# A decode block with its backward pass: the value contraction is issued ahead of the score-gradient chain, the exponential is placed first on ScalarE, and VectorE shares PSUM evacuation from the last step on

## Chip, cores and metric

The kernel runs on one core of a Trainium2 chip. The metric is the device time of one launch in microseconds (us), taken as the median of several runs; lower is better.

## What is computed

The reference is a residual block for one token of each of two sequences, `x + A(xn) + B(xn)`, and the gradients of it with respect to every input. A is attention over a cache with grouped heads, B is a gated bilinear layer.

```python
B, Sq, D = 2, 1, 576;  Hq, Hkv, Sk, Dh = 32, 16, 4096, 128;  F = 4608      # bfloat16
xn = layernorm(x)
q  = xn @ wq                                   # 32 heads; two query heads share one K/V head
p  = softmax((q . k_cache) * Dh**-0.5);  o = p @ v_cache
A  = o @ wo
B  = ((xn @ w_gate) * (xn @ w_up)) @ w_down
out = x + A + B
# returned: out, and by jax.vjp with grad_out the gradients of
# x, k_cache, v_cache, wq, wo, w_gate, w_up, w_down
```

The gradients of the caches are as large as the caches: k_cache and v_cache are 2 x 16 x 4096 x 128 values each, 32 heads of 1 MB for each of the two. Each head has to be read once and a gradient of the same size written once. Reads and writes are 92.5 MB each in all, with the weights.

## The kernel before

**Steps.** The main loop has 16 steps, n = 0 to 15. A step handles one batch row and two K/V heads with their four query rows. Four steps make a group, which shares one slice of `wq` and `wo`. A step does this:

- *Scores of K.* `slot` loads a K head (1 MB, `head_load`, L541, on SP's queue), transposes it in two halves on VectorE (`head_scores`, tile X, L141; 1.2 us a half) and multiplies it on TensorE into a PSUM tile `ps_sc`.
- *Softmax.* `by_rows` copies the scores out (VectorE, L565) and transposes them (TensorE, L569); then come the row maximum (L626), the maximum over the row group (L630, L632), the negated bias `negb` (VectorE, L635), the exponential `ex` with its row sum `z` (ScalarE, L641), the sum over the group (TensorE, L643), its reciprocal `rz` (VectorE, L645), the probabilities `pr` (L648) and their transpose `pT` (a tile rowT).
- *Scores of V.* The same with the V heads, for the gradient of the probabilities: four more half-head transposes and matmul blocks into `dp_ps`.
- *`dscores`.* `by_rows` again, the row sums `cs` (L661), the correction `cr` (L668), the score gradient `ds` (L669) and its transpose `dsT`.
- *Contractions.* `end_of_V` (L802) sums the V rows with the probabilities: 64 matmuls that read both V heads as they were loaded, a copy `o_sb` (L588), one small matmul (L591), a copy into `oT`. It needs `pT` and not `ds`. `end_of_K` (L797) does the same with `dsT` and the K heads; it is traced in the next step.
- *Outer products.* The gradients of K and V: `masked` (GpSimd, L597) spreads `pr` and `ds` into `prm` and `dsm`, `build_bd` (GpSimd, L532) spreads a query row into `bd`, and `outer_units` multiplies them in pairs of matmuls into a PSUM tile `ps_o`, evacuates each pair (1024 columns, 256 KB) into a quarter of a tile `so` and stores each full `so` (1 MB) from GpSimd's queue (L618). 16 pairs in a step are for the outer products of K and V.

Units of the gated layer (`mlp_units`, in nine of the steps) and of the gradients of `wq` and `wo` (`back_units`, after each group) wait in a list `side` and are interleaved. Their outputs pass through `ps_o` and tiles `stw`, `std`, `stt`, `sto`, `stq`, `stqt`.

**Evacuation.** `evac` (L116) sends a PSUM copy either to VectorE (L121) or to ScalarE (L124). It keeps an estimate of the load of each engine in `load`, to which `dve()` and `act()` add other work. VectorE is allowed only once `ending` is filled, which is after the last step; before that all these copies go to ScalarE.

**Order.** Instructions are put in order at build time by a list scheduler: each engine then runs its queue strictly in that order. `tc.high_priority()` lets an instruction go ahead of others that are ready at that point of the schedule. The matmuls of a `Block` are kept together (all carry the line L105).

**Buffers.** Loaded heads and weights share 12 slots (tag `nat`), output tiles share 5 (tag `st`), so a load on SP's queue waits until a contraction has freed a slot, and a copy into a new output tile waits until an earlier store has landed. PSUM has two `ps_o`, two score tiles (tag `sc`) and two small tiles (tag `m`). Once `ending` is filled, every third pair uses the two score tiles (`ps_x`) instead of a `ps_o`.

**End.** After step 15, `end_of_K`, the outer products left over, `back_units` of the last group and `final_units` (the output `out`, and the gradient of x: a chain of some ten small VectorE instructions, L835 to L873) are interleaved in the order of `side`.

Of the kernel before, what the change touches and what calls it, by code (L numbers as in the profile page):

```python
# [8 lines left out]
AF = mybir.ActivationFunctionType  # L9
# [7 lines left out]
def view(t, p0, np_, off, dims):  # L17

    (pstep, _), *_ = t.ap
    return bass.AP(t.tensor, t.offset + p0 * pstep + off, [[pstep, np_], *[list(d) for d in dims]])  # L20
# [3 lines left out]
def kernel(  # L24
# [22 lines left out]
    nc = tc.nc  # L47
# [10 lines left out]
    NIT = NGRP * Bq * 2  # L58
    NCH = Sk // P
    WW = 48 + P  # L60
    SCALE = float(Dh) ** -0.5
# [12 lines left out]
    def ps_m(shape, dtype=FP32):  # L74
        return ps.tile(list(shape), dtype, tag="m", bufs=2, name="ps_m")

    def ps_sc():
        return ps.tile([P, P], FP32, tag="sc", bufs=2, name="ps_sc")
# [3 lines left out]

    pairs_made = [0]
    ending = []

    def ps_pair():

        pairs_made[0] += 1
        if ending and pairs_made[0] % 3 == 0:
            o = [ps.tile([P, 512], FP32, tag="sc", bufs=2, name="ps_x") for _ in range(2)]  # L90
            return [t[:] for t in o], None
        o = ps_o()
        return [o[:, 0, :], o[:, 1, :]], o
# [20 lines left out]
    load = {"v": 0.0, "s": 0.0}  # L114

    def evac(out, in_, cols):  # L116
        cv = 0.16 + cols * 0.00104
        cs = 0.19 + cols * 0.00083
        if ending and load["v"] + cv < load["s"] + cs:
            load["v"] += cv  # L120
            nc.vector.tensor_copy(out=out, in_=in_)  # L121
        else:
            load["s"] += cs
            nc.scalar.copy(out, in_)  # L124
# [7 lines left out]
                evac(out(a), view_in(o[a]), cols // 2)  # L132

    def dve(us):
        load["v"] += us

    def act(us):
        load["s"] += us

    def t32(out, in_):  # L140
        nc.vector.transpose(out, in_)  # L141
# [370 lines left out]
    def build_W(st, b, s, t):  # L512
        for a in range(4):
            nc.gpsimd.tensor_copy(  # L514
                view(W[t][:], 32 * a, 32, 48 + 4 * a, [[2 * WW, 4], [WW + 2, 2], [1, 2]]),
                view(st["rep"][:], 32 * a, 32, t * 4 * GH * 2 + 8 * s + b, [[GH * 2, 4], [4, 2], [2, 2]]),
            )
# [18 lines left out]
    def small(name, shape=(P, 1), dtype=FP32, bufs=2):  # L536
        return sb.tile(list(shape), dtype, tag=name, bufs=bufs, name=name)
# [24 lines left out]
    def by_rows(t_ps):  # L562

        s_sb = small("s_sb", (P, P), FP32, 1)
        nc.vector.tensor_copy(s_sb[:].rearrange("p (a c m) -> p a c m", a=4, c=8),  # L565
                              view(t_ps[:], 0, P, 0, [[4, 4], [16, 8], [1, 4]]))
        act(0.35)
        s_ps = ps_sc()
        nc.tensor.transpose(s_ps[:], s_sb[:], identf[:])  # L569
        return s_ps  # L570
# [52 lines left out]
    def softmax(s_ps):  # L623
        s_ps = by_rows(s_ps)
        mx = small("mx")
        nc.vector.reduce_max(mx[:], s_ps[:], axis=AX.X)  # L626
        mT = ps_m([1, P])
        nc.tensor.transpose(mT[:], mx[:], identf[:])
        m4 = small("m4", (1, 4))
        nc.vector.reduce_max(m4[:], mT[0:1, :].rearrange("o (a m) -> o m a", m=4), axis=AX.X)  # L630
        nb_ps = ps_m([P, 4])
        nc.tensor.matmul(nb_ps[:], lhsT=ones[:], rhs=m4[:], start=True, stop=True)  # L632
        negb = small("negb")
        nb4 = small("nb4", (P, 4), FP32, 1)
        nc.vector.tensor_tensor_reduce(  # L635
            out=nb4[:], in0=nb_ps[:], in1=R4[:], scale=-SCALE, scalar=0.0,
            op0=ALU.mult, op1=ALU.add, accum_out=negb[:],
        )
        ex = small("ex", (P, P), FP32, 1)
        z = small("z")  # L640
        nc.scalar.activation(ex[:], s_ps[:], AF.Exp, bias=negb[:], scale=SCALE, accum_out=z[:])  # L641
        z_ps = ps_m([P, 1])
        nc.tensor.matmul(z_ps[:], lhsT=G4[:].rearrange("p a m -> p (a m)"), rhs=z[:], start=True, stop=True)  # L643
        rz = small("rz")
        nc.vector.reciprocal(rz[:], z_ps[:])  # L645

        pr = small("pr", (P, P), BF16)
        nc.vector.tensor_scalar(pr[:].rearrange("p (j c) -> p j c", c=4), view(ex[:], 0, P, 0, [[1, 32], [32, 4]]),  # L648
                                rz[:], None, op0=ALU.mult)
        pT = rowT[0][n_rows[0] % 2]  # L650
        n_rows[0] += 1
        t32(pT[:, 0:P], view(pr[:], 0, P, 0, [[1, 4], [4, 32]]))
        dve(0.3 + 0.3 + 0.3 + 0.2 + 0.2 + 0.25 + 0.25)
        act(0.5)
        return pr, pT, ex, rz

    def dscores(pr, ex, rz, dp_ps):
        dp_ps = by_rows(dp_ps)
        ds = small("ds", (P, P), BF16)
        cs = small("cs")  # L660
        nc.vector.tensor_tensor_reduce(  # L661
            out=ds[:], in0=ex[:], in1=dp_ps[:], scale=1.0, scalar=0.0,
            op0=ALU.mult, op1=ALU.add, accum_out=cs[:],
        )
        c_ps = ps_m([P, 1])
        nc.tensor.matmul(c_ps[:], lhsT=G4[:].rearrange("p a m -> p (a m)"), rhs=cs[:], start=True, stop=True)
        cr = small("cr")
        nc.vector.tensor_tensor(cr[:], c_ps[:], rz[:], ALU.mult)  # L668
        nc.vector.scalar_tensor_tensor(  # L669
            out=ds[:].rearrange("p (j c) -> p j c", c=4), in0=view(dp_ps[:], 0, P, 0, [[1, 32], [32, 4]]),  # L670
            scalar=cr[:], in1=pr[:].rearrange("p (j c) -> p j c", c=4), op0=ALU.subtract, op1=ALU.mult)
        dsT = rowT[1][n_rows[1] % 2]
        n_rows[1] += 1
        t32(dsT[:, 0:P], view(ds[:], 0, P, 0, [[1, 4], [4, 32]]))
        dve(0.3 * 2 + 0.2 + 0.25)
        return ds, dsT
# [95 lines left out]
    side = []  # L772
# [11 lines left out]
    def slot(src, t, b, l, s_ps, per, mid=None):  # L784
        n = head_load(src, b, l)
        head_scores(n, t, l % 2, s_ps, 0)
        more(2)
        if mid:
            mid()
        head_scores(n, t, l % 2, s_ps, 1)  # L790
        more(2)
        other(per)
        return n
# [6 lines left out]
    def end_of_V(st, b, s, V, pT):  # L800
        t_ps = contract(pT, V)
        nc.vector.tensor_copy(st["oT"][:, 0, 4 * s:4 * s + 4, b], t_ps[:])  # L802
        dve(0.2)

    def step(n):
        g, k = divmod(n, 4)
        return g, k // 2, k % 2
# [70 lines left out]
    final = final_units()  # L878
# [4 lines left out]
    st = group_front(0, *loaded)  # L883
# [3 lines left out]
    for n in range(NIT):  # L887
        g, b, s = step(n)
        l0 = G * g + 2 * s
        side += plan.get(n, [])[1:]  # L890
        per = max(1, -(-len(side) // 4))
        new = n + 1 < NIT and step(n + 1)[0] != g
        K, V = [], []
        if new:
            loaded = group_loads(g + 1)
        s_ps = ps_sc()
        for x in range(2):
            K.append(slot(kview, 0, b, l0 + x, s_ps, per, (lambda: end_of_K(*last[:5])) if x == 0 and last else None))
            if x == 0:
                if last:  # L900
                    outs += outer_units(last[5], last[6], last[1], G * last[0]["g"] + 2 * last[2], okview)
                    if last[0]["g"] != g:
                        side[0:0] = back_units(last[0])
                        per = -(-len(side) // 4)
                bd1 = build_bd(st, b, s, 1)
        pr, pT, ex, rz = softmax(s_ps)
        prm = masked(pr, "prm")
        if n + 1 < NIT and not new:
            build_W(st, *step(n + 1)[1:], 0)
        dp_ps = ps_sc()  # L910
        for x in range(2):
            if x == 1 and n + 1 in plan:
                plan[n + 1][0][0]()
            V.append(slot(vview, 1, b, l0 + x, dp_ps, per))
            if x == 0:
                outs += outer_units(prm, bd1, b, l0, ovview)
                bd0 = build_bd(st, b, s, 0)
                if new:
                    nxt = group_front(g + 1, *loaded)
                    build_W(nxt, 0, 0, 0)  # L920
        if n + 1 < NIT:
            build_W(nxt if new else st, *step(n + 1)[1:], 1)
        ds, dsT = dscores(pr, ex, rz, dp_ps)
        dsm = masked(ds, "dsm")
        end_of_V(st, b, s, V, pT)
        last = (st, b, s, K, dsT, dsm, bd0)
        if new:
            st = nxt
# [3 lines left out]
    end_of_K(*last[:5])  # L932
    outs += outer_units(last[5], last[6], last[1], G * last[0]["g"] + 2 * last[2], okview)
    units = back_units(last[0])
    side += final[:1] + units[:2] + final[1:] + units[2:]
    while outs or side:
        more(2)
        other(1)
# [30 lines left out]
```

## Time and profile before

| | |
|---|---|
| median of 5 runs | 499.01 us (495.48 to 500.01) |
| profiled execution: its time, its span | 502.08 us, 500.3 us |
| busy: TensorE, ScalarE, VectorE, GpSimd | 77%, 70%, 65%, 53% of the span |
| DMA: reads queue, writes queue | 48.4%, 46.7% of 16 engines' span |
| moved | 186.06 MB, mean 372 GB/s |
| one 1024-column evacuation | ScalarE 1.02 us (mean of 249); VectorE 1.22 to 1.23 us |
| load of one head, issue to landing (median) | 12.9 us (K), 16.7 us (V) |
| last 1 MB store issued, last GpSimd store issued, end | 483.0 us, 493.7 us, 500.3 us |

The profile lists for each engine what it did and, for the idle time ahead of an instruction, which other engine's work ended it. Times are counted from the start of the span. A GB/s figure for a stretch of time says what all 16 DMA engines moved in it. No compute engine is busy throughout, and the DMA rate changes from stretch to stretch, so the stages have to be read one by one.

### The profile page before, as it was taken

To read this page: it belongs to the slowest core of one execution; us is meant where nothing else is said; L and a number is where in the kernel's file an instruction comes from. 1 tells how busy PE (TensorE), PEld (TensorE's weight loads), DVE (VectorE), ACT (ScalarE), POOL (GpSimd) and SP (SyncE) were. 2 spreads that over 40 slices of the span, in tenths; PEclk is the share of its full clock that TensorE was granted. 3 is DMA by queue.
4 is the path that set the end of the run, shared out by engine and by line. 5 is a ranking of instruction groups with operands and counts; after the bars stand their busy time and mean duration, and the time that the engine had idled before them with its cause. 6 is when DMAs were issued, how large, how long until landed. Compare 5 with 4: busy or idle time off the path is not lost.

```text
span 500.3 us, 16989 instructions
## 1 busy us (share of the span) xinstructions
PE 383.1 (77%) x7344; PEld 260.1 (52%) x7417; DVE 327.1 (65%) x680; ACT 348.4 (70%) x439; POOL 264.6 (53%) x404
## 2 busy tenths in 40 slices
PE   2777879867878888488998868668888678888843
PEld 1665656544655565366665446445656446564510
DVE  6786784942858686465787565566678474884383
ACT  4143867848757877477986768757787678899843
POOL 3245356743646474456547346547557246587613
PEclk9865988979989898878999879978999878999995
DMA  7998999999799999989999999999999999996765
GB/s 252 384 399 311 355 416 397 420 420 404 273 389 391 421 415 402 422 330 392 383 418 405 419 419 352 418 395 395 366 384 408 414 422 332 420 390 236 261 257 189
DMA packets 52900, 186.06 MB, mean 372 GB/s; under 512 B 4141, under 2 KB 19129, under 8 KB 44633
## 3 DMA queue, kind: packets, MB, share of 16 engines
q1 hardware_dynamic: 28392, 92.49, 48.4%
q0 software_dynamic: 24432, 92.48, 46.7%
q8 instruction: 58, 0.95, 0.7%
q14 instruction: 18, 0.14, 0.1%
HBM read 92.48 MB, written 92.48 MB: 370 GB/s over the span
## 4 chain that ended last, share of the span: by engine, by line
PE 32%; DMA 26%; DVE 12%; ACT 11%; issue 8%; POOL 4%; another core or an unknown queue 0%; POOLq 0%; ACTq 0%; SPq 0%; DVEq 0%
DMA out_dram<-so 14%; PE ps_o L105 13%; DMA kv<-in_A_k_cache_dram 9%; PE ps_m L105 9%; ACT so L124 9%; PE ps_sc L105 5%; DVE X L141 5%; DMA wgu<-in_B_w_gate_dram 3%; DVE Xw L141 2%; POOL prm L597 1%; PE ps_m L591 1%; ACT std L124 1%; POOL bd L532 1%; POOL out_dram L764 1%; ACT stw L124 1%
## 5 line engine op out<-in xcount | busy, mean ns | idle before, releaser
L124 ACT CAST so<-ps_o 128x1024 bf16<-128x1024 f32 x249 | 238.8, 1023 | 67.3 <-PE ps_o L105 26.0
L141 DVE STREAM_TRANSPOSE X<-kv 128x1024 f32<-128x1024 f32 x128 | 157.4, 1233 | 38.8 <-DMA kv<-in_A_k_cache_dram 16.0
L105 PEld LDWEIGHTS <-X 128*128 128x128 bf16 x2048 | 81.7, 103 | 33.0 <-DVE X L141 14.6
L105 PE MATMUL ps_sc<-W,X 128*128 128x64 bf16 (+1 forms) x2048 | 89.8, 200 | 7.7 <-DVE X L141 4.6
L105 PE MATMUL ps_o<-bd,prm 128*128 128x512 bf16 x212 | 74.5, 428 | 16.6 <-ACT so L124 5.6
L618 POOL DMA_DIRECT2D out_dram<-so x64 | 50.2, 784 | 69.7 <-ACT so L124 49.5
L105 PE MATMUL ps_o<-bd,dsm 128*128 128x512 bf16 x219 | 71.9, 399 | 10.1 <-ACT so L124 7.2
L532 POOL TENSOR_TENSOR bd<-dense,maskq 128x1024 bf16<-128x1024 bf16 x32 | 60.6, 1894 | 15.1 <-DVE dense L529 10.9
L124 ACT CAST stw<-ps_o 128x1024 bf16<-128x1024 f32 x36 | 34.7, 1016 | 16.2 <-PE ps_o L105 6.7
L124 ACT CAST std<-ps_o 128x576 bf16<-128x576 f32 x36 | 21.4, 644 | 32.9 <-PE ps_o L105 27.1
L105 PEld LDWEIGHTS <-prm 128*128 128x128 bf16 x256 | 22.5, 105 | 32.4 <-issue 20.1
L514 POOL COPY W<-rep 32x16 bf16<-32x16 bf16 x128 | 25.2, 197 | 26.6 <-PE ps_sc L105 18.8
L105 PE MATMUL ps_m<-kv,rowT 128*32 128x128 bf16 x2048 | 36.8, 226 | 1.5 <-issue 1.3
L597 POOL TENSOR_TENSOR prm<-pr,maskc 128x1024 bf16<-128x1024 bf16 x16 | 30.3, 1892 | 14.2 <-DVE pr L648 13.5
L105 PEld LDWEIGHTS <-dsm 128*128 128x128 bf16 x256 | 21.6, 103 | 27.5 <-issue 20.5
L105 PEld LDWEIGHTS <-rowT 128*32 128x32 bf16 x2048 | 30.6, 100 | 5.9 <-issue 4.4
L597 POOL TENSOR_TENSOR dsm<-ds,maskc 128x1024 bf16<-128x1024 bf16 x16 | 30.4, 1901 | 5.7 <-DVE ds L669 5.4
L105 PEld LDWEIGHTS <-Wdy 128*128 128x128 bf16 x306 | 22.8, 110 | 7.9 <-DVE Xo L141 2.9
L124 ACT CAST sto<-ps_o 128x576 bf16<-128x576 f32 x27 | 16.5, 650 | 13.7 <-PE ps_o L105 12.4
L141 DVE STREAM_TRANSPOSE Xw<-wgu 128x1152 f32<-128x1152 f32 x18 | 24.2, 1354 | 2.0 <-PE ps_sc L105 2.0
L105 PEld LDWEIGHTS <-xnr 32*128 32x128 bf16 (+1 forms) x440 | 12.8, 97 | 20.3 <-issue 15.6
L414 POOL DMA_DIRECT2D out_dram<-stw x18 | 13.9, 772 | 16.2 <-ACT stw L124 16.2
(186 smaller groups left out, 553.6 us busy)
## 6 DMA issues: line engine op xcount, KB each, us to landing
out_dram<-so POOLq DMA_DIRECT2D x64, 1024.0 KB, 12.4
kv<-in_A_k_cache_dram SPq DMA_DIRECT2D x32, 1024.0 KB, 12.9
kv<-in_A_v_cache_dram SPq DMA_DIRECT2D x32, 1024.0 KB, 16.7
out_dram<-stw POOLq DMA_DIRECT2D x18, 512.0 KB, 10.7
wd<-in_B_w_down_dram SPq DMA_DIRECT2D x9, 576.0 KB, 5.3
out_dram<-std POOLq DMA_DIRECT2D x9, 576.0 KB, 9.0
wo<-in_A_wo_dram SPq DMA_DIRECT2D x4, 1152.0 KB, 12.8
wgu<-in_B_w_gate_dram SPq DMA_DIRECT2D x9, 512.0 KB, 14.4
```

Of the source, the lines that this page charges most:

```text
L105: ins = nc.tensor.matmul(*args, **kwargs)
L124: nc.scalar.copy(out, in_)
L141: nc.vector.transpose(out, in_)
L414: nc.gpsimd.dma_start(out[0:512, f0:f0 + FS].rearrange("(c p) n -> p c n", p=P), st[:])
L514: nc.gpsimd.tensor_copy(view(W[t][:], 32 * a, 32, 48 + 4 * a, [[2 * WW, 4], [WW + 2, 2], [1, 2]]), view(st["rep"][:], 32 * a, 32, t * 4 * ...
L532: nc.gpsimd.tensor_tensor(bd[:], view(dense[:], 0, P, 0, [[Dh, 2], [0, 4], [1, Dh]]), view(maskq[:], 0, P, 0, [[0, 2], [1, 4], [0, Dh]]), ...
L591: nc.tensor.matmul(t_ps[:], lhsT=o_sb[:], rhs=RV[:].rearrange("p x r -> p (x r)"), start=True, stop=True)
L597: nc.gpsimd.tensor_tensor(m[:], view(rows[:], 0, P, 0, [[0, 8], [1, P]]), view(maskc[:], 0, P, 0, [[1, 8], [0, P]]), ALU.mult)
L618: nc.gpsimd.dma_start(oview[b, :, :, l0 + x].rearrange("a m n -> m a n"), st[:].rearrange("p a c d -> p a (c d)"))
L764: nc.gpsimd.dma_start(out_5[r0:r0 + 4 * P, :].rearrange("(h p) n -> p h n", p=P), m["so"][:])
```

## The change

Four edits. First, in `softmax` the exponential is issued with high priority. Second, `end_of_V` is traced ahead of `dscores` and `masked`. Third, a second flag `both` is set at the start of step 15, with the load estimates set to zero; from there on `evac` may choose VectorE, and `dve()` no longer adds to VectorE's estimate once `ending` is filled. Fourth, at the end the last unit of `final_units` (the gradient of x) is placed behind the four pairs of units that make the gradient of `wo` (`outer_o`), instead of ahead of them.

```diff
-        if ending and load["v"] + cv < load["s"] + cs:
+        if both and load["v"] + cv < load["s"] + cs:
             load["v"] += cv
             nc.vector.tensor_copy(out=out, in_=in_)
...
     def dve(us):
-        load["v"] += us
+        if not ending:
+            load["v"] += us
...
-        nc.scalar.activation(ex[:], s_ps[:], AF.Exp, bias=negb[:], scale=SCALE, accum_out=z[:])
+        with tc.high_priority():
+            nc.scalar.activation(ex[:], s_ps[:], AF.Exp, bias=negb[:], scale=SCALE, accum_out=z[:])
...
         side += plan.get(n, [])[1:]
+        if n == NIT - 1:
+            both.append(1)
+            load["v"] = load["s"] = 0.0
...
+        end_of_V(st, b, s, V, pT)
         ds, dsT = dscores(pr, ex, rz, dp_ps)
         dsm = masked(ds, "dsm")
-        end_of_V(st, b, s, V, pT)
...
-    side += final[:1] + units[:2] + final[1:] + units[2:]
+    side += final[:1] + units[:2] + final[1:3] + units[2:6] + final[3:] + units[6:]
```

More of the change, by code (lines that the diff above doesn't have):

```diff
@@ L84 @@
     ending = []
+    both = []
     def ps_pair():
```

## The prediction

> **What bounds the kernel now.** I read the page first: shares of the engines, then the DMA rate in 40 slices.
>
> ```profile
> PE 383.1 (77%) x7344; PEld 260.1 (52%) x7417; DVE 327.1 (65%) x680; ACT 348.4 (70%) x439; POOL 264.6 (53%) x404
> ...
> DMA  7998999999799999989999999999999999996765
> GB/s 252 384 399 311 355 416 397 420 420 404 273 389 391 421 415 402 422 330 392 383 418 405 419 419 352 418 395 395 366 384 408 414 422 332 420 390 236 261 257 189
> ```
>
> No compute engine is full, while DMA is near its best rate (415 to 422 GB/s) in many slices. 186 MB at 415 GB/s are 448 us of a 500.3 us span. What can be won lies where the rate is below that: in dips about once or twice a group, and in the last 50 us. The windows view of those stretches:
>
> ```profile
> 48.00:60.00 12.00, 11.11 (x278) 7.99 (x284) 8.30 (x16) 10.39 (x13) 4.00 (x8) 0.98 0.88 333
> 128.00:142.00 14.00, 10.86 (x279) 8.28 (x280) 12.96 (x24) 9.45 (x10) 8.23 (x20) 1.00 0.80 278
> 220.00:228.00 8.00, 7.37 (x223) 5.38 (x224) 5.57 (x13) 7.03 (x9) 6.48 (x5) 1.00 0.79 264
> 304.00:312.00 8.00, 6.74 (x173) 4.88 (x174) 3.20 (x6) 7.37 (x10) 3.87 (x6) 1.00 1.01 330
> 360.00:372.00 12.00, 11.31 (x279) 7.73 (x272) 8.33 (x17) 9.97 (x11) 6.69 (x8) 1.00 0.96 351
> 420.00:428.00 8.00, 6.57 (x169) 4.87 (x171) 2.83 (x8) 7.38 (x9) 4.56 (x6) 1.00 0.94 318
> 448.00:500.30 52.30, 32.90 (x446) 16.26 (x450) 28.15 (x58) 33.96 (x46) 25.11 (x28) 0.86 0.67 242
> ```
>
> The last column is GB/s. Against 415, a stretch of length w loses w x (1 - rate/415): 2.4, 4.6, 2.9, 1.6, 1.9, 1.9, and 21.8 us in the last. Why the dips are there is told by the waits of SP's queue, which issues the loads (waited for: total, times, longest):
>
> ```profile
> SPq L337 <- PE ps_m L105: 56.4, 5, 20.1
> ...
> SPq L541 <- PE ps_m L105: 32.4, 13, 7.0
> ```
>
> The load of `wd` and the heads behind it wait for a contraction (tile ps_m) to free a slot: in step 3 `wd` is issued at 134.75, just after the V contraction began (133.63). So I asked what holds that contraction, in the timeline of PE in step 3:
>
> ```profile
> 115.25 0.38 PE L632 MATMUL ps_m<-m,ones 1*128 1x4 f32 x2
> 116.02 0.59 PE L105 MATMUL ps_o<-bd,prm 128*128 128x512 bf16 x2 [0.40 <-ACT so L124]
> ...
> 122.44 0.59 PE L105 MATMUL ps_o<-bd,dsm 128*128 128x512 bf16 x2 [0.32 <-ACT so L124]
> 122.87 0.30 PE L643 MATMUL ps_m<-z,G 128*128 128x1 f32 x2
> ```
>
> Pairs for the outer products stand between the two small matmuls of the softmax, 0.92 us each because ScalarE evacuates them, and the exponential (122.20) stands behind the same copies on ScalarE, although its bias was ready at 115.75. Step 15 has the same picture; the timelines of ACT and DVE:
>
> ```profile
> 453.39 7.43 ACT L124 CAST so<-ps_o 128x1024 bf16<-128x1024 f32 x8 [0.24 <-PE ps_o L105]
> 460.67 0.41 ACT L641 ACTIVATE ex<-ps_sc,negb 128x128 f32<-128x128 f32 x1
> ...
> 453.74 0.08 DVE L635 DVE_READ_ACCUMULATOR2_ANT negb<- 128x1 f32 x1
> ...
> 461.21 0.29 DVE L661 CUSTOM_DVE_ANT_0 ds<-ex,ps_sc 128x128 bf16<-128x128 f32 x1 [5.92 <-ACT ex L641]
> ```
>
> The exponential could start at 453.8 and starts at 460.67; VectorE idles 5.92 us for it. From about 450 no head is left to load, and the rate falls: the end is set by chains.
>
> **Part 1, the exponential.** By the timelines it is late behind its bias by 6.45 us in step 3, 1.8 in 6, 4.8 in 9, 1.75 in 10, 4.2 in 13, 1.8 in 14, 6.9 in 15, and at most 1.2 elsewhere. In the order of instructions of the changed kernel it stands 4 copies earlier in step 3, 2 in steps 6, 9 and 13, 3 in 7, 10, 11 and 14, 8 in 15, and 2 or 3 later in steps 2 and 4. Step 3: 4 x 0.92 = 3.7 us. Steps 9 and 13: the first of four 0.55 us copies waits for a store until 294.52 and 411.45, and stays ahead; 2 x 0.55 = 1.1 us each. Steps 6, 10, 14: 1.1 to 1.8. Step 15: the whole 6.8. The copies it overtakes come 0.6 us later (0.41 and the read of the sum, 0.24); the queue behind them has that slack, since ScalarE idles 30% of the span. Steps 2 and 4 lose at most 2 and 3 copies of 0.6 to 1 us; in 4 the copies precede a bias that comes late anyway (153.71, behind a load), so I take nothing.
>
> **Part 2, the V contraction.** In the changed order the pairs between the bias matmul and the V contraction fall from 17 to 6 in step 3, from 12 to 3 in steps 7 and 11, from 7 to 3, 5, 5 in 6, 9, 13. At 0.92 us a pair, less what the exponential still holds, the V slots come free 7 to 8 us sooner in 3, 7, 11 and, by the rows of step 9 (the sum's matmul behind 3 pairs instead of 5, so `rz` 2.1 us sooner, and `pT` made ahead of a 1.4 us transpose instead of behind it), about 3.4 us sooner in 9 and 13: loads issued at 302.94 and 419.45 move to 299.5 and 416. But something is moved back. On VectorE `cr`, `ds` and `dsT` now stand behind three to six transposes of the next heads (step 6: 1 to 5 before `dsT`; step 10: 2 to 5; 1.2 us each), so the K contraction and the two slots that it frees come later: 1 to 2 us in steps 0, 2, 3, 5, 6, 8, 10, 12, about 12 us summed, and 1 to 3 us sooner in 4, 7, 9, 11, 13. GpSimd's `dsm` and the K outer products follow it; SP's order of issue is unchanged.
>
> What this is worth before 411 us: the dips there lose 13.4 us. A load takes 12.9 us from issue to landing, though 1 MB at 415 GB/s is 2.5, so some 10 us of queued transfers cover a slot that comes 1 or 2 us late; outside the dips an earlier slot wins nothing for the same reason. Best case: the dips fed by V slots close (2.9 + 1.6 + 1.9) and a third of that of step 3 (1.6): -8. Worst: the late K slots meet an empty queue in most of their steps: +10. I take -2, near nothing, since V sooner and K later alternate.
>
> From 411.45 ScalarE no longer waits for stores of a backlog, and steps 13 and 14 are a chain: -1.1 for the exponential, -3.4 for V, -1 for K, later ordering against it in 14: I take -2 (between -3.4 and +1).
>
> [...]
>
> **Part 3, VectorE evacuates from step 15 on.** The changed order has six more copies on VectorE: four `so` of 1.22 us and one `ps_x` of 0.65, a `sto` of 0.74 instead of one of 0.44, one `stqt` of 0.68, in all 6 us with the overlap of neighbours taken off. `exp` to `Wm` (the step that starts the last group's gradients) took 460.67 to 471.43. It now starts 6.8 us sooner, and two `so` copies stand inside the chain, between the V and K copies into `oT`, in place of two `ps_x` behind it: +1.0. So `Wm` at 465.6. From there VectorE had 16.9 us of work and 4.0 of gaps to its last copy (492.37). It gets 5.1 more, and fills most gaps: 22.0 + 1.3 = 23.3, last copy at 488.9, that is -3.5 us. With no gap left -5; with all of them -1. The rest (7.9 us from the last copy to the end of the span: two stores, their landing, the close) stays. ScalarE's list ends sooner than VectorE's, so VectorE sets the end. On GpSimd `prm`, `bd` and the preparation of the last units (0.66 + 0.66 + 2.30 us) now stand ahead of three stores around 445 to 451; the slots of these are wanted only near 457, so I take nothing; without that cover it is 3.6 us.
>
> **Part 4, the order of the last units.** The gradient of x goes behind the `sto` copies, so the two `sto` stores leave before the small chain, not at 488.54. They are not the last transfer: inside part 3.
>
> **Sum.** -2 - 2 - 3.5 = -7.5: 502.08 becomes 494.6 for the profiled execution, which lies 3.1 above the median. On the median: 499.0 - 7.5 = 491.5; for this case alone 486 to 494.
>
> **Rivals.**
> - *The dips close.* For: every dip lies behind a late contraction. Against: K slots come later in eight steps. -8 - 3.4 - 4.5: 483.
> - *VectorE eats the gain.* For: its estimate no longer counts its own work at the end, and it gets 5 us more behind `Wm`; two copies of 1.2 us sit inside the chain. Against: 15 us of gaps after 455. Parts 1 to 3 give -2: 497.
> - *K slots late: slower.* VectorE runs in order, so `cr` waits behind transposes that themselves wait for a load that waits for a slot. For: VectorE waits 16 us in all for K loads now. Against: these heads were issued 20 us or more before use outside the dips. It decides once six of the eight late steps lose 2 us each: +12, less 5.5 kept at the end: 505.5.
> - *The exponential blocks ScalarE*, standing at its head with the bias not ready. It did so in steps 0, 2, 4, 7 and 11 already (late by at most 0.2): a few us, inside the range.
>
> **How the numbers follow.** Forecast 0.45, dips close 0.17, VectorE eats it 0.25, slower 0.13. Range 482 to 501: both nearest rivals are in, and 2 in 10 outside, most of it above. A measurement of this kernel tells about 1% from no change (494.0 to 504.0). Faster by over 1%: 0.6; within 1%: 0.28; slower: 0.12.
>
> **What would show it.** The exponential of step 15 within 1 us of its bias, and VectorE's idle time for `ex` gone; `wd` issued 7 us sooner after the bias of step 3, and K contractions 1 to 2 us later behind `rz` in steps 6 and 10; rates above 300 in the six windows; VectorE's last copy about 8 us before the end of the span, with ScalarE done before it. Wrong if VectorE shows new waits for K loads ahead of `cr`, if the six windows stay below 300, or if the last VectorE copy is no sooner, counted from the last bias.

## The result, and the profile after

The changed kernel took 497.58 us (median of 36 runs, 491.60 to 504.01), the kernel before in the same comparisons 499.38 (71 runs). The ratio is 0.9952, with a 95% interval of 0.9933 to 0.9970: 2.4 us faster, where 7.5 were forecast. The ratio takes only the runs within 1.5% of the fastest of their kernel, so it is not the quotient of the two medians. The profiled execution took 497.36 us (span 495.5), which is its median; that of before lay 2.7 above its own, so the two spans differ by more than the kernels do, and the ratios are what counts below. Sums over a profile, here and below, are those of one execution each.

The page of the changed kernel, with the shares of the engines and the transfer rows in 40 slices:

```profile
PE 386.0 (78%) x7338; PEld 264.1 (53%) x7417; DVE 332.2 (67%) x686; ACT 343.9 (69%) x433; POOL 265.3 (54%) x404
...
DMA  8999999999999999997999999999899999977695
GB/s 248 380 390 379 415 408 401 418 420 406 412 412 410 420 410 413 418 415 267 367 413 384 419 414 306 419 413 405 295 410 400 393 417 392 401 276 266 257 341 191
```

The dips of before have gone from where they were and stand elsewhere: 267, 306 and 295 GB/s. The windows view shows both, first the stretches of the prediction (the last one up to the new end), then three new ones:

```profile
48.00:60.00 12.00, 10.48 (x268) 7.34 (x269) 7.84 (x17) 9.46 (x12) 6.36 (x13) 1.00 1.01 414
128.00:142.00 14.00, 11.76 (x276) 7.80 (x277) 11.03 (x22) 12.17 (x15) 8.08 (x16) 1.00 1.02 417
220.00:228.00 8.00, 6.30 (x71) 4.46 (x71) 1.73 (x9) 4.57 (x7) 0.80 (x1) 0.50 0.95 362
304.00:312.00 8.00, 5.75 (x71) 3.62 (x73) 4.14 (x9) 5.70 (x9) 2.57 (x4) 1.00 1.02 391
360.00:372.00 12.00, 11.69 (x224) 6.97 (x224) 9.28 (x14) 11.68 (x14) 5.92 (x11) 1.00 1.02 408
420.00:428.00 8.00, 6.93 (x102) 4.60 (x103) 5.50 (x11) 7.40 (x11) 2.80 (x5) 1.00 1.01 387
448.00:495.50 47.50, 30.78 (x416) 15.60 (x419) 30.57 (x61) 28.74 (x39) 22.59 (x25) 0.86 0.76 275
...
230.00:240.00 10.00, 8.64 (x201) 6.05 (x203) 8.78 (x17) 8.95 (x10) 8.50 (x17) 1.00 0.72 227
296.00:304.00 8.00, 6.64 (x211) 5.26 (x210) 3.44 (x9) 5.98 (x7) 6.18 (x10) 0.90 0.84 266
350.00:360.00 10.00, 8.88 (x219) 6.31 (x220) 8.57 (x18) 8.97 (x10) 7.55 (x15) 1.00 0.79 280
```

Adding up the slices of the GB/s row (each rate by a 40th of the span), before had moved 55.2 MB by 150 us and after 58.6; by 425 us it was 164.1 and 166.2; by 450 us 174.2 and 174.1. The lead of 8 us of transfer that stands at 150 us, after step 3, is all given back before the end.

Where a part of it goes is seen in step 7. Its row maximum `mx` is done at 212.5 instead of 227.6, but the bias only at 223.8 instead of 231.1: 11.3 us for what took 3.5. The timelines of ScalarE, TensorE and VectorE there:

```profile
220.05 1.93 ACT L125 CAST so<-ps_o 128x1024 bf16<-128x1024 f32 x2 [5.25 <-DMA out_dram<-so]
...
221.11 1.01 PE L106 MATMUL ps_o<-bd,prm 128*128 128x512 bf16 x2 [4.95 <-ACT so L125]
221.92 0.42 PE L630 MATMUL ps_m<-identf,mx 128*1 128x128 f32 x1
...
222.37 0.28 DVE L632 TENSOR_REDUCE m<-ps_m 1x4 f32<-1x128 f32 x1 [6.16 <-PE ps_m L630]
```

Read from the top: ScalarE has no output tile free until a store lands, the pair on TensorE has no PSUM tile `ps_o` free until ScalarE copies, the transpose of the row maximum stands behind that pair in TensorE's queue, and VectorE waits 6.16 us for it. In the waits view this kind of wait grew from 7.4 us (3 times) to

```profile
ACT so L125 <- DMA out_dram<-so: 28.6, 9, 5.3
```

(total, times, longest), while VectorE's waits for K loads, 16.0 us before, fell to 1.3. Waits for loads were traded for waits for stores.

### The profile page after: what moved, and what is told of

It reads as the page before. It is cut to its first block, busy times and chain, and to the rows that moved or that the text cites. A ratio compares the mean times of both kernels' runs of the same rounds, so it can differ in the third digit from the quotient of the medians.

```text
span 495.5 us, 16979 instructions
## 1 busy us (share of the span) xinstructions
PE 386.0 (78%) x7338; PEld 264.1 (53%) x7417; DVE 332.2 (67%) x686; ACT 343.9 (69%) x433; POOL 265.3 (54%) x404
## 4 chain that ended last, share of the span: by engine, by line
DMA 32%; PE 25%; DVE 12%; ACT 11%; issue 9%; POOL 6%; DVEq 0%; POOLq 0%; ACTq 0%
DMA out_dram<-so 29%; PE ps_o L106 9%; PE ps_m L106 9%; ACT so L125 9%; DVE X L143 5%; PE ps_sc L106 3%; DMA out_dram<-stw 3%; POOL bd L534 2%; POOL dsm L599 2%; DVE Xw L143 1%; ACT sto L125 1%; POOL prm L599 1%; ACT std L125 1%; DVE so L122 1%; PE ps_m L646 1%
## 5 line engine op out<-in xcount | busy, mean ns | idle before, releaser
L125 ACT CAST so<-ps_o 128x1024 bf16<-128x1024 f32 x245 | 235.0, 1019 | 88.1 <-DMA out_dram<-so 28.6
L143 DVE STREAM_TRANSPOSE X<-kv 128x1024 f32<-128x1024 f32 x128 | 156.1, 1227 | 25.4 <-PE ps_sc L106 16.2
L106 PEld LDWEIGHTS <-X 128*128 128x128 bf16 x2048 | 80.7, 102 | 25.7 <-DVE X L143 9.9
L106 PE MATMUL ps_sc<-W,X 128*128 128x64 bf16 (+1 forms) x2048 | 88.6, 199 | 4.9 <-DVE X L143 3.5
L106 PE MATMUL ps_o<-bd,dsm 128*128 128x512 bf16 x210 | 67.3, 391 | 12.9 <-ACT so L125 9.5
L106 PE MATMUL ps_m<-kv,rowT 128*32 128x128 bf16 x2048 | 42.0, 246 | 3.0 <-DVE rowT L143 2.7
L106 PEld LDWEIGHTS <-rowT 128*32 128x32 bf16 x2048 | 35.7, 111 | 12.7 <-DVE rowT L143 7.6
L125 ACT CAST std<-ps_o 128x576 bf16<-128x576 f32 x36 | 21.8, 646 | 18.9 <-PE ps_o L106 15.2
L106 PEld LDWEIGHTS <-Wdy 128*128 128x128 bf16 x306 | 24.3, 115 | 6.6 <-DVE Xo L143 2.9
L106 PEld LDWEIGHTS <-xnr 32*128 32x128 bf16 (+1 forms) x440 | 13.8, 99 | 23.1 <-issue 19.6
L590 DVE COPY o_sb<-ps_m 128x128 f32<-128x128 f32 x32 | 8.8, 275 | 23.9 <-PE ps_m L106 23.7
```

The costliest lines, as they stand in the source:

```text
L106: ins = nc.tensor.matmul(*args, **kwargs)
L590: nc.vector.tensor_copy(o_sb[:], o_ps[:])
```

## Experiments

Ratios are to the kernel before, runs of the same chip, with the 95% interval; 0.001 is 0.5 us. The first theories were S (the output slots: stores land later beside the earlier reads, ScalarE and TensorE's queue stand) and K (the K contraction, now behind the V contraction and the transposes, frees its slots late).

**One part at a time.** Each kernel has one part of the change.

```diff
# e1: before, and
+        with tc.high_priority():
+            nc.scalar.activation(ex[:], ...)
# e2: before, and
+        end_of_V(st, b, s, V, pT)
         ds, dsT = dscores(pr, ex, rz, dp_ps)
         dsm = masked(ds, "dsm")
-        end_of_V(st, b, s, V, pT)
# e3: before, with `both`, `dve` and the order of the last units as changed
# e4: before, with the edits of e1 and e2
```

> Only the exponential is issued with high priority; the V contraction and the end are as before. Theory S (stores): a sooner chain lets loads go out sooner, these take DMA time from the stores, and ScalarE then waits for output slots, so what is won in the middle is given back; only step 15, with no loads left, keeps it. S expects -1 to -2 us on the median (ratio 0.996 to 0.998). Theory K (late K slots): the loss comes from cr and dsT standing behind transposes, which this kernel has only where the order shifts by itself; the exponential then keeps its gain in steps 3, 9, 13, 14, 15: -3 to -6 us (0.988 to 0.994). Noise alone: within 0.5 us.

> Only end_of_V is traced ahead of dscores. S expects about 0 (-1 to +1 us): wd is issued 5 to 10 us sooner in steps 3, 7 and 11, the rate dips of before close, new dips open some 90 us later with ScalarE waiting for out_dram<-so several times as long as the 7.4 us of before. K expects +2 to +5 us (1.004 to 1.01), with VectorE waiting for K loads ahead of cr.

> Only the end: VectorE may evacuate from step 15 on, and the last unit goes behind the sto copies; the exponential and the V contraction as before. Both theories expect most of the end's gain only if the exponential does not matter there: with the late exponential of step 15 kept, copies shared by two engines ahead of it let it start some 3 us sooner, so -1 to -3 us (0.994 to 0.998). If the gain of the end comes from the exponential alone, 0.

> Exponential and V contraction as in the changed kernel, the end (evac, side) as before. S expects -1 to 0 us: the chain of step 15 is 6 to 8 us sooner but ScalarE alone carries the copies to the end. K expects +1 to +4 us. If the sum of the parts holds, e4 plus e3 gives the 0.9952 of the whole change.

| | median us | ratio |
|---|---|---|
| e1, exponential alone | 501.84 | 1.0063 [1.0031, 1.0094] |
| e2, V contraction alone | 502.58 | 1.0074 [1.0042, 1.0107] |
| e3, end alone | 495.83 | 0.9958 [0.9923, 0.9993] |
| e4, exponential and V contraction | 498.27 | 0.9999 [0.9960, 1.0037] |
| all | 497.58 | 0.9952 [0.9933, 0.9970] |

The end holds the whole gain. In the middle each edit alone costs 3 to 4 us, and both together nothing. Neither theory holds throughout: e2 has K's time, but S's waits (ScalarE waits 23.2 us for stores, VectorE only 5.6 for K loads), e4 has S's time, and e1 went against both. In its profile step 4 is 9 us sooner (`mx` at 137.2 instead of 146.2), and a wait of VectorE in step 5 takes all of it (the bias at 177.3, before 177.5):

```profile
171.90 1.25 DVE L141 STREAM_TRANSPOSE X<-kv 128x1024 f32<-128x1024 f32 x1 [7.11 <-DMA kv<-in_A_v_cache_dram]
```

That head's load was issued 9.3 us sooner than before (148.76 instead of 158.07), but it landed little sooner: the loads of heads issued between 140 and 180 us take 25.6 us to land (median), where they took 16.2. Why this ends in a loss of 3 us and not at zero, the runs don't tell.

**Output slots, and the stores themselves.** f1 and f2 have six output slots instead of five, and eleven load slots instead of twelve. f3 and f4 store half of each gradient block.

```diff
# f1 (changed kernel), f2 (before): at each place
-tag="st", bufs=5      -tag="nat", bufs=12
+tag="st", bufs=6      +tag="nat", bufs=11
# f3 (changed kernel), f4 (before)
-nc.gpsimd.dma_start(oview[b, :, :, l0 + x].rearrange("a m n -> m a n"),
-                    st[:].rearrange("p a c d -> p a (c d)"))
+nc.gpsimd.dma_start(oview[b, :, :, l0 + x].rearrange("a m n -> m a n")[:, 0:2],
+                    st[:].rearrange("p a c d -> p a (c d)")[:, 0:2])
```

> The changed kernel with six output slots in place of five (tag st), and eleven load slots in place of twelve, which pays for the room. Theory S (output slots): the earlier contractions fetch heads sooner, stores land later beside them (stw 14.8 us against 10.7), ScalarE stands with all five output slots out and TensorE's pairs and the row maximum stand behind it. Then ScalarE's wait for out_dram<-so falls from 28.6 us to under 15, mx to negb in steps 7 and 11 falls from 11 to 12 us to under 6, and the time against the kernel before goes to 0.985 or below, less what the missing load slot costs; against the kernel before with the same slots it is 0.985 or below. Theory K (late K slots): the output slots change nothing, the missing load slot makes late K slots dearer: time against the kernel before 1.00 to 1.02, and 1.00 or above against the kernel before with the same slots. Theory D (the DMA rate alone: a dip that closes opens again a step later, whoever waits): waits for stores fall, but another wait takes their place, and the time stays within 0.3% of 0.995 in both comparisons.

> The kernel before with the same trade: six output slots, eleven load slots. Its ScalarE waits only 7.4 us for out_dram<-so in the middle. Theory S: little to win, 0.99 to 1.00 against the kernel before plus the price of the missing load slot. Theory K: SP waits longer for slots, VectorE's 16.0 us of waits for K loads grow to 20 or more, 1.00 to 1.015. Theory D: 1.00 to 1.01, the price of a load slot.

> The changed kernel, with half of each gradient block of K and V left unstored (the other half of out_2 and out_3 isn't written); 33.5 MB of 186 MB less to move, 81 us less of transfer at 415 GB/s. Theory S: stores land in under 9 us, output slots are never all out, so ScalarE's waits for out_dram<-so fall below 5 us, mx to negb is under 5 us in every step, and the whole of the earlier V contraction is kept: against the kernel before with half stores it is faster by 6 to 12 us (0.975 to 0.985). Theory K: the late K slots still cost, and with the queue of transfers shorter even more: 0 to 4 us slower than the kernel before with half stores. Theory D: DMA is no longer the bound in either, both are set by chains, and the difference is that of the chains: the end's 3 us and some of the steps', 3 to 6 us.

> The kernel before, with half of each gradient block of K and V left unstored (the other half of out_2 and out_3 isn't written). All theories: 30 to 60 us faster than the kernel before, since the middle runs at 380 to 420 GB/s of a mixture in which the stores are 33.5 MB less; what counts is the distance of the changed kernel with the same stores: S 6 to 12 us below this one, K 0 to 4 us above it, D 3 to 6 us below it.

Measured: f1 501.03 (1.0041 [1.0002, 1.0079]), f2 515.37 (1.0347 [1.0299, 1.0396]); f3 462.37 (0.9250 [0.9203, 0.9297]), f4 464.91 (0.9293 [0.9239, 0.9348]), 2.5 us apart: the size of the end's gain, within intervals as wide as that. In f1 ScalarE's wait for stores is down to 1.3 us and nothing is won; with half of those stores gone, the changed middle still has no gain over the old one. Of S's signs the waits came, and so did the distance to the kernel before with the same slots (0.97 between f1 and f2). But that distance comes from f2: the kernel before loses 16 us where the changed one loses 4. Whether that is the load slot or the output slot, the next runs decide.

**Load slots alone, and less work on TensorE.** g1 and g2 take only the load slot away. g3 and g4 keep the slots and leave out half of the score matmuls. Theory L: two slots given back sooner are worth nothing while twelve cover the loads. Theory P: TensorE, busy 28 of 31 us where a group begins, takes the lead.

```diff
# g1 (changed kernel), g2 (before)
-tag="nat", bufs=12
+tag="nat", bufs=11
# g3 (changed kernel), g4 (before)
-                for c8 in range(8):
+                for c8 in range(4):
-                        start=first, stop=(x == 1 and be == 3 and c8 == 7),
+                        start=first, stop=(x == 1 and be == 3 and c8 == 3),
```

> The changed kernel with eleven load slots in place of twelve and its five output slots. With six output slots and eleven load slots it took 501.0 us. Theory L (the slots of loads: the earlier V contraction gives two slots back sooner, and with twelve slots the transfers queued already cover nearly all of that): the load slot alone makes the difference, 499 to 504 us. Theory S (output slots): the sixth output slot had saved some of the 28.6 us for which ScalarE waits; without it 505 to 511 us.

> The kernel before with eleven load slots and its five output slots. With six output slots and eleven load slots it took 515.4 us. Theory L: 512 to 518 us, 9 to 16 us above the changed kernel with the same slots. Theory S: it hardly waits for stores, so 513 to 518 us as well, but only 3 to 9 us above the changed kernel, which needs the sixth output slot.

> The changed kernel, with half of the matmuls of the score contraction left out (four of eight column groups; the other four get no scores): about 2.5 us of TensorE less in each step, all loads, stores, copies and transposes as they were. Theory P (in the stage that begins a group, from the bias of steps 3, 7 and 11 to that of the next step, TensorE is busy for 28 of 31 us, and a lead of the loads is lost there): these stages fall to 28 to 29 us, the windows there (338 and 362 GB/s) rise above 380, and it is faster than the kernel before by 8 to 12 us (0.976 to 0.984). Theories L and S (TensorE is not what holds these stages): 0 to 3 us faster than the changed kernel, 0.989 to 0.996 against the kernel before.

> The kernel before, with half of the matmuls of the score contraction left out (four of eight column groups; the other four get no scores). Theory P: its stages are held by the late V contraction more than by TensorE's work, so it wins less than the changed kernel: 2 to 5 us (0.990 to 0.996), and the changed kernel with the same edit is 5 to 9 us faster. Theories L and S: 0 to 4 us faster than the kernel before, and the distance to the changed kernel with the same edit stays at 2 to 3 us.

Measured: g1 500.69 (1.0027 [0.9988, 1.0066]), g2 515.96 (1.0356 [1.0298, 1.0415]): as with six output slots, so the output slot changes neither and the load slot does it all. With that theory S falls: f1 has hardly a wait for stores left (1.3 us) and is no faster than g1. These waits are where the lead goes, not what takes it. With eleven load slots the change is worth 15.3 us, with twelve 2.4. The waits of g2 show what the old order then meets (16.0 us for K loads and 1.0 for V loads with twelve slots):

```profile
DVE X L141 <- DMA kv<-in_A_k_cache_dram: 36.2, 9, 11.8
...
DVE X L141 <- DMA kv<-in_A_v_cache_dram: 12.2, 4, 5.0
```

g3 gave 497.80 (0.9971 [0.9941, 1.0002]) and g4 496.10 (0.9932 [0.9899, 0.9965]): with this edit the changed kernel is not faster than the kernel before, which no theory expected, though the intervals overlap. Theory P's time is wrong, and the stages behind the biases of steps 7 and 11 still take 31.3 and 31.6 us (31.4 and 32.0 in the changed kernel), although their windows rose to 390 and 399 GB/s. This is the GB/s row of g3:

```profile
GB/s 256 385 398 381 419 413 394 420 414 372 410 416 409 421 409 409 419 414 386 381 412 408 419 392 416 415 334 406 408 411 408 421 416 418 218 186 228 257 341 191
```

The dips are all but closed: 48 to 411 us lose 8 us against 415 GB/s, where before lost 18 and after 16 (from the same slices). By 425 us g3 has moved 169.3 MB, 5.2 more than before, and its last head is asked for 20 us sooner, as SP's timelines show, before and g3:

```profile
421.69 1.45 SPq L541 DMA_DIRECT2D kv<-in_A_v_cache_dram  x2
```

```profile
401.95 1.02 SPq L543 DMA_DIRECT2D kv<-in_A_v_cache_dram  x2
```

Yet by 450 us it has moved 174.4 MB, no more than before's 174.2, and it ends no sooner than the changed kernel. The lead is lost in step 14. Its row maximum is done at 411.9, 15.8 us sooner than in the changed kernel, but its bias only at 433.2 (434.5 there). ScalarE's and TensorE's timelines show the wait of step 7 again, with the transpose of the row maximum behind pairs:

```profile
418.92 1.93 ACT L125 CAST so<-ps_o 128x1024 bf16<-128x1024 f32 x2 [5.34 <-DMA out_dram<-so]
...
431.29 0.27 PE L630 MATMUL ps_m<-identf,mx 128*1 128x128 f32 x1
```

So closing the dips by 8 to 10 us of transfer won some 3 us (g4) or nothing (g3). One rival is left: the mean clock granted to TensorE is lower in g3 and g4 (0.841 and 0.835, the changed kernel and the kernel before 0.886; last section), which may have taken a part of the gain; no run tells.

**Work out of the last steps, and priority for the chain to `ds`.** h1 to h3 move units of the gated layer from the last steps to steps 3 and 7; h4 gives the chain to `ds` priority, which was to put it ahead of the next heads' transposes. Theory E: the steps behind the last load run at their own pace and give back any lead. Theory T: only the sum of the transfers counts.

```diff
# h1 (changed kernel), h2 (before); h3 (changed kernel): (0, 1, 2, 3, 5, 6, 7, 9, 10)
-    plan = dict(zip((0, 1, 2, 5, 6, 9, 10, 13, 14), ...
+    plan = dict(zip((0, 1, 2, 3, 5, 6, 9, 10, 13), ...
# h4: changed kernel, and
-        ds, dsT = dscores(pr, ex, rz, dp_ps)
+        with tc.high_priority():
+            ds, dsT = dscores(pr, ex, rz, dp_ps)
```

> The changed kernel with the last unit of the feed-forward gradients (weights of 1.8 MB to read and 1.8 MB of gradients to store, some 7 us of ScalarE copies) done in step 3 instead of step 14. Theory E (a lead of the loads is given back between 420 and 450 us, where the steps after the last load run at the pace of their copies, pairs and stores, whatever came earlier): step 14 gets shorter by 5 us or more, step 3 longer by less, 2 to 6 us faster than the changed kernel: 0.983 to 0.991 against the kernel before. Theory T (only the sum of the transfers counts, wherever they stand): within 1.5 us of the changed kernel, 0.992 to 0.998. Theory L (slots of loads): the two more slots that step 3 needs at the start of a group cost 2 to 6 us: 0.999 to 1.008.

> The kernel before with the same move of the last feed-forward unit from step 14 to step 3. Theory E: 1 to 5 us faster than before (0.990 to 0.998), since its step 3 has the late V contraction, which the unit's loads now meet. Theory T: 0.997 to 1.003. Theory L: slower than the changed kernel's step, 1.005 to 1.02.

> The changed kernel with the last two feed-forward units moved: from steps 13 and 14 to steps 3 and 7. Theory E: twice as much leaves the end, 4 to 9 us faster than the changed kernel: 0.977 to 0.987 against the kernel before. Theory T: 0.992 to 0.998. Theory L: 1.003 to 1.02.

> The changed kernel with the chain from the V scores to ds and its transpose put ahead of the transposes of the next heads on VectorE, so that the K contraction no longer waits behind them. Theory K (the K slots that come 1 to 2 us late in eight steps eat what the V slots win): 2 to 5 us faster than the changed kernel, 0.985 to 0.991 against the kernel before, and K contractions 1 to 2 us sooner behind rz in steps 6 and 10. Theories E and T (earlier slots are worth nothing with twelve of them): within 1.5 us of the changed kernel, 0.992 to 0.998.

Measured: h1 502.67 (1.0077 [1.0041, 1.0112]), h2 507.77 (1.0193 [1.0149, 1.0236]), h3 514.51 (1.0313 [1.0271, 1.0354]). Theory T is out, and these moves go as L said, h3 beyond its range: at the start of a group two more slots are dear, and dearer in the old order (9.6 us) than in the new (6.2 us over the changed kernel). E is not decided by them, since what they took from the end they paid for in slots.

h4 took 494.16 us (0.9924 [0.9897, 0.9952]), the lowest median of the kernels that do all of the work, 1.4 us below the changed one by the ratios, with intervals that overlap. That is in the range of E and T, not in K's. Its waits view and its windows over the three new dips:

```profile
DVE X L143 <- DMA kv<-in_A_k_cache_dram: 16.3, 4, 6.6
ACT so L125 <- DMA out_dram<-so: 4.9, 3, 2.1
```

```profile
230.00:240.00 10.00, 8.98 (x178) 6.31 (x181) 10.00 (x18) 9.15 (x11) 4.95 (x12) 1.00 1.04 411
296.00:304.00 8.00, 4.86 (x54) 3.11 (x55) 3.49 (x6) 5.65 (x9) 2.00 (x4) 1.00 1.04 399
350.00:360.00 10.00, 9.18 (x195) 6.26 (x197) 8.10 (x17) 9.12 (x10) 5.90 (x8) 1.00 1.03 421
```

ScalarE's waits for stores go from 28.6 us to 4.9 and the three dips close, while VectorE's waits for K loads are back, 16.3 us instead of 1.3.

**The middle alone, with priority for the chain to `ds`.** i1 is e4 and i2 is e2 with the edit of h4. Rival H: the V contraction alone fails because it stands in TensorE's queue and waits for a late exponential.

> The kernel before with the exponential first and the V contraction first, its end as it was, and with the chain from the V scores to ds and its transpose put ahead of the transposes of the next heads. Without that last edit it stood at 0.9999. Theory K (the late ds and K contraction eat what the V slots win): 0.993 to 0.9975, and ScalarE's waits for out_dram<-so fall from 15.5 us to under 8. Theory E (earlier slots are worth nothing, whichever they are): 0.9985 to 1.002.

> The kernel before with the V contraction first and the same chain ahead of the transposes, but the exponential where it was; its end as it was. Without the chain's edit it stood at 1.0074. Theory K: the loss came from the late ds and K contraction, so 0.998 to 1.003. Rival H (the V contraction stands in TensorE's queue and waits for an exponential that is still behind copies, so it needs the exponential's edit whatever ds does): 1.005 to 1.010. Theory E: 1.005 to 1.010 as well.

Measured: i1 494.57 (0.9919 [0.9890, 0.9949]), against e4's 0.9999: 4.0 us. i2 497.75 (0.9975 [0.9939, 1.0011]), against e2's 1.0074: 4.9 us. H and E fall. K's times nearly came, both a little beyond its ranges on the fast side. Its reason does not hold, because the edit does not do what was expected of it. Between `rz` and `dsT` VectorE still makes as many transposes of the next heads: 39 over the 16 steps in i1, 36 in e4, 30 in the kernel before. And the last matmul of the K contraction, which frees the slots, ends no sooner behind `rz`: summed over the 16 steps 177 us in i1 and 170 in e4, 173 in h4 and 177 in the changed kernel, 134 in the kernel before. In steps 6 and 10 it is 11.4 and 11.0 us in h4, 9.8 and 9.5 in the changed kernel. ScalarE's waits for stores in i1 are 13.0 us, where under 8 were expected.

What holds the chain is seen in step 6, in the timelines of VectorE (`cs`) and TensorE. The matmul with `cs` is the small one that sums over the group, ahead of `cr`. The one of `kv,rowT` is the V contraction, the one of `RV,o_sb` its small matmul. First the kernel before, then the changed one, then i1:

```profile
215.74 0.08 DVE L661 DVE_READ_ACCUMULATOR2_ANT cs<- 128x1 f32 x1
...
217.52 0.57 PE L666 MATMUL ps_m<-cs,G 128*128 128x1 f32 x2
...
219.93 1.08 PE L105 MATMUL ps_m<-kv,rowT 128*32 128x128 bf16 x64
```

```profile
204.53 0.07 DVE L664 DVE_READ_ACCUMULATOR2_ANT cs<- 128x1 f32 x1
...
205.37 1.08 PE L106 MATMUL ps_m<-kv,rowT 128*32 128x128 bf16 x64
...
208.96 0.39 PE L593 MATMUL ps_m<-RV,o_sb 128*128 128x4 f32 x2 [1.08 <-DVE o_sb L590]
209.21 0.36 PE L669 MATMUL ps_m<-cs,G 128*128 128x1 f32 x2
```

```profile
206.35 0.08 DVE L662 DVE_READ_ACCUMULATOR2_ANT cs<- 128x1 f32 x1
...
211.70 1.08 PE L105 MATMUL ps_m<-kv,rowT 128*32 128x128 bf16 x64
...
213.77 0.39 PE L591 MATMUL ps_m<-RV,o_sb 128*128 128x4 f32 x2
214.01 0.36 PE L667 MATMUL ps_m<-cs,G 128*128 128x1 f32 x2
```

In the kernel before the matmul with `cs` stands ahead of the V contraction in all 16 steps. In the changed kernel, e2, e4, h4, i1 and i2 it stands behind it and behind its small matmul in all 16, whatever priority the chain has. From `cs` to its matmul 12.0 us pass in the kernel before, summed over the steps, 62.9 in the changed one, 74.5 in h4 and 77.8 in i1; `cr`, `ds` and `dsT` come after that. Behind `dsT` the K contraction then waits less than before (7.1 us summed instead of 14.9), so it is `dsT` that makes it late. Outer-product pairs between the two contractions, some 46 instead of 13 by the matmuls recorded, hold it by more than 0.6 us in step 2 alone, there by 4.5 us.

So priority for the chain is shown to be worth 4.0 and 4.9 us with the old end; with the new one it is 1.4, within the noise. How it wins them is not shown. In i1 the V contraction ends later behind `rz` than in e4 (85 us summed instead of 68) and the K contraction no sooner; in i2 V is 7 us later than in e2 and K 6 us sooner.

## Why the prediction was right and wrong

**The end: right in size.** ScalarE's and VectorE's timelines in step 15:

```profile
452.48 0.37 ACT L644 ACTIVATE ex<-ps_sc,negb 128x128 f32<-128x128 f32 x1
...
452.04 0.07 DVE L637 DVE_READ_ACCUMULATOR2_ANT negb<- 128x1 f32 x1
...
454.19 0.28 DVE L664 CUSTOM_DVE_ANT_0 ds<-ex,ps_sc 128x128 bf16<-128x128 f32 x1
...
463.66 0.41 DVE L288 TENSOR_TENSOR Wm<-ps_m,mask 128x256 bf16<-128x256 f32 x1
...
487.56 1.39 DVE L122 CAST stqt<-ps_o 64x512 bf16<-64x512 f32 x2
```

The exponential starts 0.4 us behind its bias and VectorE no longer idles for it. Bias to `Wm` is 11.6 us where 11.8 were worked out. `Wm` to the last copy is 25.3, not 23.3: VectorE fills fewer gaps than taken. The rest after it is 6.6 instead of 7.9. From bias to the end that is 43.5 us instead of 46.6: -3.1 in the profile for a term of -3.5, with two misses, +2.0 and -1.3, that partly cancel. By the ratios e3 has -2.1 us (-3.8 to -0.4), and the changed kernel stands 2.3 below e4. Where the gain comes from was not as worked out. Part 3 drew it from the exponential, 6.8 us sooner, and counted VectorE's copies as its cost. But e4, with the exponential first and ScalarE alone, takes 45.8 us from bias to end, and e3, with the copies shared and no priority for the exponential, 42.6. So the shared copies carry it, or the order of the last units, which e3 has too and no run separates. Beside priority for the chain to `ds` no gain of the end is seen (h4 0.9924, i1 0.9919), but 1.5 us either way is within these intervals.

**"Before 411 us" and "steps 13 and 14": wrong.** -2 and -2 were taken; the two edits measure 0.0 us together (e4, -2.0 to +1.8). The mechanism of the gain was there: `wd` is issued at 121.01, 8.1 us behind the bias of step 3 instead of 18.9, and all six windows are above 300. The signs came and the time did not. Two steps of the working failed.

- *The K side of part 2, in place and size.* It was put at 1 to 2 us in eight steps, 12 us summed, from the transposes on VectorE that `dsT` stands behind. In the profile the last matmul of the K contraction ends 3.1 and 4.1 us later behind `rz` in steps 6 and 10, over 2 us later in eleven of the 16 steps, and 43 us later summed over all of them. The wait that was left out is on TensorE, where the matmul with `cs` now stands behind the V contraction: 62.9 us instead of 12.0. Whether this lateness is what cancels V's gain stays open. i1 has as much of it and is 4.0 us faster than e4. That i1 comes to the -4 of the two terms is therefore no proof of their working. What is shown is that the gain depends on more than when slots come free: on the load slots (15.3 us with eleven) and on the priority of the chain to `ds` (4.0 us).
- *Reading a dip as time to be won.* The first part of the prediction looked for the gain where the rate is below 415 GB/s. g3 closes the dips and wins nothing over the changed kernel: its lead goes in step 14, to the queues of TensorE and ScalarE (its lower clock, 0.841 instead of 0.886, aside). The half-store kernels are 2.5 us apart like the full ones.

**Rivals.** "VectorE eats the gain" named 497, and 497.6 came, but by another way: VectorE took 2.0 us more behind `Wm` than worked out, while the middle, not VectorE, lost the rest. "The dips close" happened at the places named and bought nothing. "K slots late" had its condition met, more than 2 us in eleven steps, without the loss of 12 us that it drew from that. VectorE's waits for K loads ahead of `cr`, which were to show it, fell from 16.0 to 1.3 us; `cr` waited for TensorE instead. "The exponential blocks ScalarE" was left at a few us. e1, where it moves alone, is 3.1 us slower, for a reason that stays open.

## What to carry to other kernels

When a consumer is moved ahead so that its buffer comes free sooner, look in every engine's queue for small instructions of the next consumer's chain that now stand behind it. Here it was one matmul with a single column, and its wait grew from 12.0 to 62.9 us. An edit of the priority has to be checked in the same place: here it left that matmul where it was. Ask first whether buffers are what is waited for: the same edits of the middle were worth some 13 us with eleven load slots (15.3 less the end's 2.4, if that is the same there) and nothing with twelve. And a dip that closes need not be a gain: here steps 7 and 14 lost the lead again behind pairs and output tiles (g3, its dips all but closed, stands at 0.9971, the changed kernel at 0.9952).

## What the runs showed of the hardware that was not expected

Half of the score matmuls left out made TensorE only little less busy. This is the page of g3:

```profile
PE 383.0 (77%) x6393; PEld 236.3 (48%) x6393; DVE 335.9 (68%) x686; ACT 343.5 (69%) x433; POOL 265.1 (54%) x404
```

It has all of its 6393 matmuls. The page of the changed kernel has records of 7338 out of 7417, so its 386.0 us are too few; e1 to e4, with all 7417, have 391.3 to 394.3. From e4 to g3 the score matmuls fell from 89.0 to 56.3 us and TensorE's busy time from 394.3 to 383.0, a third of that. The rest came back elsewhere, the pairs of the outer products taking 449 and 403 ns a matmul instead of 419 and 392. The mean granted clock is 0.841, where the changed kernel has 0.886 (in the kernel before with the same edit 0.835 instead of 0.886). The row of the changed kernel from 220 to 228 us has a granted clock of 0.50, behind the 4.95 us for which TensorE waited in step 7. That this wait lowered it is not shown, and no run shows why the mean is lower in g3 and g4. So the 32.7 us of score matmuls left out were worth 11.3 us of TensorE's busy time here, nothing in the time of the changed kernel (g3 0.9971, the changed kernel 0.9952) and some 3 us in that of the kernel before (g4 0.9932).

The price of a slot is steep at one size: the twelfth load slot is worth 17 us to the kernel before (515.96 and 498.94 in the same comparison) and 4 us to the changed one, and beside eleven load slots the sixth output slot is worth nothing to either (501.03 with it and 500.69 without, 515.37 and 515.96).
